# Issuing two weight loads earlier on GpSimd in a linear-attention and feed-forward kernel

## The chip, the cores and the metric

The kernel runs on one core of a Trainium2 chip. The metric is the time of one execution on the device, in microseconds, as the median of several runs. A profiled execution has two numbers: its own time, and its span, which goes from the first instruction's start to the last one's end.

## The reference, cut to what matters

Linear attention with decay runs over 4 batches, 8 heads, 768 positions and head size 64, in blocks of 64 positions that hand a 64x64 state from one to the next. Its output, taken as 3072 tokens of 512 values, goes through a feed-forward layer with a leaky gate.

```python
for b in range(nb):                      # blocks of 64 positions
    intra = np.einsum('bhic,bhjc->bhij', qb, kb) * Dmask[None]
    intra = np.einsum('bhij,bhjd->bhid', intra, vb)
    inter = np.einsum('bhid,bhde->bhie', qb * lam_pow[None], kv_state)
    out[:, :, sl] = intra + inter
    kb_dec = kb * rev_pow[None]
    kv_state = lam_block[None, :, None, None] * kv_state + np.einsum('bhsd,bhse->bhde', kb_dec, vb)
...
h = x @ w_in                             # x: 3072 x 512, w_in: 512 x 2048
g = np.maximum(h, 0.0) + alpha * np.minimum(h, 0.0)
return (g @ w_out).astype(np.float32)    # w_out: 2048 x 512
```

## The kernel before, in words

**Units and chunks.** The tokens are worked on in six chunks `c`. A chunk holds 256 positions of two batches (`bi` 0 and 1), so 512 tokens. The attention of a chunk is cut into four units, one for each batch and each half of the heads (`hh`). Units are numbered through: units 0 to 3 belong to chunk 0, units 4 to 7 to chunk 1, and so on. "The third and fourth unit" are units 2 and 3.

**What a unit does.** `turn` transposes queries and keys on TensorE, `turned` copies them out of PSUM, `decayed` multiplies queries by the decay, `key_decayed` makes the decayed keys, `cast` makes 16-bit copies of the keys or queries. `cluster(old, new)` is a burst of small matmuls: scores and state increments of the new unit, outputs of the old one. `masked` multiplies the scores by the decay mask on VectorE. `aged` (L686, always on GpSimd) multiplies a state by its decay into the tile `old`, and `state` (L675 on ScalarE or L677 on VectorE) adds the increment. `out_of` (on ScalarE) copies the attention output of a unit into `xT`, the input of the feed-forward layer.

**The feed-forward layer.** `up(c, f, bi, slot)` makes 128 of the 2048 hidden values for the tokens of a chunk: four matmuls (L705) into one of three PSUM banks; `bi` other than None takes half of the tokens. `below` (L716, ScalarE) and `gate` (L728, VectorE) turn the bank into the tile `g`, and only then is the bank free for a later `up`. `down` (L738) multiplies `g` by `w_out_sb`.

**Loads.** Three queues issue transfers. GpSimd issues those that change 32-bit floats to 16-bit ones: the values `vh`, some of the queries `qh`, and the weights, `w_in_sb` by `load_win` (L116) and `w_out_sb` by `load_wout` (L122). In the profile these are queue q0, software_dynamic. SyncE issues the keys `kraw` and some queries in 32 bits (L83); they are queue q1, hardware_dynamic. ScalarE issues the stores of the output. `load_win(c0, n)` brings n columns of `w_in`, for `up` with f from c0/128 on. `load_wout(f0, n)` brings n of the sixteen blocks of 128 rows of `w_out`. `hold` is a tiny VectorE write into a key tile, which makes the load of this tile wait until VectorE has reached that point.

**The order.** The program is a list written out by hand, one call after another, from line 771 to line 1164; from there a loop weaves the remaining chunks together. Each engine takes its own instructions in the order of this list and waits at the first that is not ready. Around the change GpSimd's order before is: `aged(1, 1)`, `decayed(3)`, `aged(9, 0)`, `aged(2, 1)`, `aged(10, 0)`, `aged(3, 1)`, `load_win(1536, 512)`, `aged(11, 0)`, `load_wout(0, 4)`, `load16("q", 1, 0)`, `load16("v", 2, 0)`, `key_decayed(5)`, `load16("v", 1, 0)`, `key_decayed(4)`, `key_decayed(6)`, and further loads. SyncE issues the keys of chunk 1, `load("k", 1, 0)` for units 4 and 5 and `load("k", 1, 1)` for units 6 and 7, behind `hold("k", 1, 0)` at line 854. Their first readers outside GpSimd are `cast(4, "k", "A")` on ScalarE (line 909), `cast(5, "k", "V")` on VectorE (line 911) and `cast(6, "k", "A")` on ScalarE (line 921), each of which stands among the `below` and `gate` calls of chunk 0.

Of the kernel before, what the change touches and what calls it, by code (L numbers as in the profile page):

```python
# [11 lines left out]
def kernel(  # L12
# [102 lines left out]
    def load_win(c0, n):  # L115
        nc.gpsimd.dma_start(  # L116
            out=w_in_sb[:, :, ds(c0, n)],
            in_=moe_w_in[:, ds(c0, n)].rearrange("(g p) f -> p g f", p=128),
        )

    def load_wout(f0, n):
        nc.gpsimd.dma_start(  # L122
            out=w_out_sb[:, ds(f0, n), :],
            in_=moe_w_out[ds(f0 * 128, n * 128), :].rearrange("(f p) d -> p f d", p=128),
        )
# [111 lines left out]
    def mask_of(hl, hh):  # L237

        m = dmask[:, hl, ds(2 * hh, 2)]
        x = [list(y) for y in m.ap]  # L240
        return bass.AP(tensor=m.tensor, offset=m.offset, ap=[x[0], x[1], [64, 2], [1, L]])
# [124 lines left out]
    def bank(slot, name):  # L366
        return ps.tile([128, CH], fp32, tag=f"b{slot}", name=name)
# [84 lines left out]
    def turn(n):  # L452

        t = T[n]
        tp = t["tp"] = ps.tile([128, 2, 2, 2, L], fp16, tag="tk", name="tp")
        for x in (1, 0):
            src = half(n, "qk"[x])
            for e in range(2):
                for hp in range(2):
                    if x == 1 or "qk16" in t:  # L460
                        nc.tensor.transpose(  # L461
                            tp[:, x, e, hp, :], src[:, e, ds(2 * hp, 2)].rearrange("p l d -> p (l d)"), ident
                        )
                    else:
                        for hl in range(2):
                            nc.tensor.transpose(  # L466
                                tp[ds(hl * 64, 64), x, e, hp, :], src[:, e, hp + 2 * hl], ident
                            )
# [145 lines left out]
    def masked(n, hl=None):  # L614
        t = T[n]
        hh = units[n][2]
        if hl is not None:
            t.setdefault("sm", {})[hl] = sm_pool.tile([128, 2, 2, L], fp16, tag=f"sm{hl}", name=f"sm{hl}")
            nc.vector.tensor_tensor(  # L619
                out=t["sm"][hl],  # L620
                in0=t["s"][:, hl].rearrange("p (h x j) -> p h x j", h=2, x=2),
                in1=mask_of(hl, hh),
                op=ALU.mult,
            )
        else:

            t["sm"] = sm_pool.tile([128, 2, 2, L], fp16, tag="sm0", name="sm0")
            nc.vector.tensor_tensor(
                out=t["sm"],
                in0=t["s"][:, :, 0 : 4 * N].rearrange("p l (e x) -> p l e x", e=2),  # L630
                in1=nmask[:, ds(4 * hh, 4)]
                .rearrange("p (l h) j -> p l (h j)", l=2)
                .unsqueeze(2)
                .to_broadcast([128, 2, 2, 2 * N]),
                op=ALU.mult,
            )

    def out_of(n, eng="A"):
        c, bi, hh = units[n]
        if c not in XT:  # L640
            XT[c] = xt_pool.tile([128, NHP, 2, 2, L], fp16, tag="xT", name="xT")
        x = XT[c][:, ds(2 * hh, 2), :, bi, :].rearrange("p h e (a j) -> p a (h e) j", a=2)
        if T[n]["acc"] is not None:
            copy_on(eng, x, T[n]["acc"][:, :, 0:256].rearrange("p a (he j) -> p a he j", j=64))
        else:
            for a in range(2):
                copy_on(eng, x[:, a], T[n]["part"][a][:, 0:256].rearrange("p (he j) -> p he j", j=64))


    def follows(n, a):  # L650

        c, bi, hh = units[n]
        step = L // N if c < FIRST else 1
        b, i = 2 * (c % 2) + bi, 4 * (c // 2) + a * step
        if (b, hh, i + step) not in R:
            state_tile(b, hh, i + step)
        return R.get((b, hh, i)), R.get((b, hh, i + step))

    def state(n, a):
        before, then = follows(n, a)  # L660
        c, bi, hh = units[n]
        if then is None:
            return
        if c >= FIRST:
            for hp in range(2):
                nc.vector.scalar_tensor_tensor(  # L666
                    out=then[:, hp, :],
                    in0=before[:, hp, :],
                    scalar=nrdecay[:, 2 * hh + hp : 2 * hh + hp + 1],
                    in1=T[n]["kv"][a % 2][:, a // 2, hp, :],  # L670
                    op0=ALU.mult,
                    op1=ALU.add,
                )
        elif before is None:
            nc.scalar.activation(then, T[n]["kv"][a][:, 0], AF.Copy)  # L675
        else:
            nc.vector.tensor_tensor(out=then, in0=T[n]["kv"][a][:, 0], in1=T[n]["old", a], op=ALU.add)  # L677

    def aged(n, a):

        before, then = follows(n, a)
        if then is None:
            return
        hh = units[n][2]
        x = T.setdefault(n, {})["old", a] = half_pool.tile([128, 2, D], fp32, tag=f"old{a}", name=f"old{a}", bufs=4)
        nc.gpsimd.tensor_tensor(  # L686
            out=x,
            in0=before,
            in1=rdecay[:, ds(2 * hh, 2)].unsqueeze(2).to_broadcast([128, 2, D]),
            op=ALU.mult,  # L690
        )
# [8 lines left out]
    def up(c, f, bi, slot):  # L700
        n = CH if bi is None else W
        h_ps = HP[c, f, bi] = bank(slot, "h_ps")
        for gi in range(NHP):
            x = XT[c][:, gi]
            nc.tensor.matmul(  # L705
                h_ps[:, 0:n] if bi is None else h_ps[:, 0:n].rearrange("p (e j) -> p e j", e=2),
                lhsT=w_in_sb[:, gi, ts(f, 128)],
                rhs=x.rearrange("p e b j -> p (e b j)") if bi is None else x[:, :, bi, :],
                start=(gi == 0),
                stop=(gi == NHP - 1),  # L710
            )

    def below(c, f, bi):
        n = CH if bi is None else W
        m = M[c, f, bi] = m_pool.tile([128, CH], fp32, tag="m", name="m")
        nc.scalar.activation(m[:, 0:n], HP[c, f, bi][:, 0:n], AF.Relu, scale=-1.0)  # L716

    def gate(c, f, bi):
        n = CH if bi is None else W
        if (c, f) not in G:  # L720
            G[c, f] = g_pool.tile([128, 2, 2, L], fp16, tag=f"g{f}", name=f"g{f}")
        g, m, h_ps = G[c, f], M.pop((c, f, bi)), HP.pop((c, f, bi))
        if bi is None:
            g, mv, hv = g.rearrange("p e b j -> p (e b j)"), m, h_ps
        else:
            g = g[:, :, bi, :]
            mv, hv = (y[:, 0:n].rearrange("p (e j) -> p e j", e=2) for y in (m, h_ps))
        nc.vector.scalar_tensor_tensor(  # L728
            out=g, in0=mv, scalar=oma[:, f : f + 1], in1=hv, op0=ALU.mult, op1=ALU.add
        )  # L730
# [115 lines left out]
    aged(8, 0)  # L846
    state(1, 0)
    aged(1, 1)
    masked(1, 1)
    turn(3)  # L850
    fill(2)
# [18 lines left out]
    cluster(2, 3, True)  # L870
    gate(0, 0, 0)
    aged(10, 0)
    up(0, 1, 0, 2)
    out_of(2, "A")
    masked(3, 0)
# [3 lines left out]
    gate(0, 1, 0)  # L879
    aged(3, 1)  # L880
    cluster(3, None)
    load_win(1536, 512)
    state(3, 1)
    up(0, 2, 0, 2)
    out_of(3, "A")
# [1 line left out]
    aged(11, 0)  # L887
    below(0, 2, 0)
    up(0, 0, 1, 1)
    load_wout(0, 4)  # L890
    below(0, 3, 0)
    gate(0, 2, 0)
    below(0, 0, 1)
# [401 lines left out]
```

## Time and profile before

| | |
|---|---|
| median of 3 runs | 221.33 us (219.97 to 222.4) |
| the profiled execution's own time | 221.9 us |
| its span | 220.1 us, so 1.8 us lie around it |
| mean granted TensorE clock | 0.988 |
| TensorE busy | 211.8 us (96%) |
| VectorE, ScalarE, GpSimd busy | 127.1, 111.6, 95.9 us |
| DMA | 28.44 MB; q0 35.6% and q1 31.0% of the sixteen engines' time |

The profile is of one execution. Times in timelines count from the start of the span. The share of TensorE is nearly the whole span, so a change is worth only what it does to the few waits of TensorE, and to its clock. The DMA engines are full for the first 70 us, which is where the two moved loads lie; after that they have room.

### The profile page before, as it was taken

Reading aid. Unit: us, or ns where it says so; the run is one execution under the profiler, and the core shown is the slowest. Engines: PE = TensorE matmul, PEld = TensorE weight load, DVE = VectorE, ACT = ScalarE, POOL = GpSimd, SP = SyncE. Lnnn points to the kernel's source line nnn. Section 1 sums busy time; section 2 is a strip of 40 time slices with the busy share of each in tenths; the row PEclk is TensorE's granted clock in tenths of the full one; section 3 lists DMA queues with packets and bytes.
Section 4 is the critical chain, followed back from the end, with each engine's and each line's share of the span. In section 5 each row is a group of like instructions: output and inputs, shape, how many; then the busy total and the mean of one; then the engine's idle time right before and its main releaser. Section 6 shows DMA issues by size and latency. Waiting matters only on the chain.

```text
span 220.1 us, 5893 instructions
## 1 busy us (share of the span) xinstructions
PE 211.8 (96%) x2463; PEld 114.6 (52%) x2463; DVE 127.1 (58%) x260; ACT 111.6 (51%) x209; POOL 95.9 (44%) x146
## 2 busy tenths in 40 slices
PE   8988899899999999999999999999999999999992
PEld 8777544556665545454545444444444444444461
DVE  3988577666887787464667566556755254443000
ACT  4762585744655564646664545555445434443120
POOL 7874796553998770776596243620100000000000
PEclk9999699999999999999999999999999999999998
DMA  4999999999998599299269995236011001100221
GB/s 118 244 193 232 192 159 183 202 171 196 299 229 199 85 219 118 74 184 172 74 89 217 180 229 130 64 82 71 27 51 48 17 35 48 48 38 13 95 92 53
DMA packets 71194, 28.44 MB, mean 129 GB/s; under 512 B 52080, under 2 KB 68224, under 8 KB 71168
## 3 DMA queue, kind: packets, MB, share of 16 engines
q0 software_dynamic: 26592, 8.65, 35.6%
q1 hardware_dynamic: 40800, 13.11, 31.0%
q10 hardware_dynamic: 3776, 6.31, 8.0%
q8 instruction: 19, 0.31, 0.6%
q14 instruction: 7, 0.06, 0.1%
HBM read 27.28 MB, written 6.29 MB: 153 GB/s over the span
## 4 chain that ended last, share of the span: by engine, by line
PE 91%; ACT 2%; DVE 2%; POOL 2%; issue 1%; POOLq 0%
PE h_ps L705 38%; PE o_ps L738 32%; PE o_ps L760 6%; PE acc L538 3%; PE s L586 2%; PE op_fill L380 2%; PE acc L558 2%; PE tp L466 2%; PE tp L461 1%; PE acc L603 1%; ACT qkT L392 1%; PE mk_ps L267 1%; POOL vh L83 0%; PE s L603 0%; DVE less L245 0%
## 5 line engine op out<-in xcount | busy, mean ns | idle before, releaser
L728 DVE SCALAR_TENSOR_TENSOR g<-m,oma,h_ps 128x512 f16<-128x512 f32 (+1 forms) x106 | 73.2, 696 | 64.9 <-ACT m L716 63.5
L705 PE MATMUL h_ps<-xT,w_in_sb 128*128 128x512 f16 (+1 forms) x424 | 98.1, 364 | 0.2
L716 ACT ACTIVATE m<-h_ps 128x512 f32<-128x512 f32 (+1 forms) x106 | 59.0, 557 | 57.4 <-PE h_ps L705 55.5
L738 PE MATMUL o_ps<-w_out_sb,g 128*128 128x512 f16 x320 | 81.2, 379 | 0.0
L705 PEld LDWEIGHTS <-w_in_sb 128*128 128x128 f16 x424 | 40.4, 99 | 41.1 <-issue 1.2
L738 PEld LDWEIGHTS <-g 128*128 128x128 f16 x320 | 30.9, 98 | 35.8
L749 ACT ACTIVATE o_sb<-o_ps 128x512 f32<-128x512 f32 (+1 forms) x25 | 14.5, 580 | 18.8 <-PE o_ps L760 11.1
L619 DVE TENSOR_TENSOR sm<-s,dmask 128x512 f16<-128x512 f32 x32 | 21.2, 683 | 1.8 <-PE s L586 1.8
L392 ACT ACTIVATE xT<-acc 128x512 f16<-128x512 f32 x22 | 13.1, 597 | 16.8 <-PE acc L558 9.6
L686 POOL TENSOR_TENSOR old<-R,rdecay 128x128 f32<-128x128 f16 x24 | 9.6, 408 | 26.3 <-DVE R L677 15.7
L444 POOL TENSOR_TENSOR kdec<-kraw,kdecay 128x256 f16<-128x256 f32 x30 | 18.4, 638 | 1.5 <-DMA kraw<-in_k_dram 0.8
L494 POOL TENSOR_TENSOR qdT<-qkT,nqdecay 128x512 f16<-128x512 f16 x8 | 9.3, 1165 | 21.5 <-DMA qkT<-qk 17.8
L494 POOL TENSOR_TENSOR qdT<-qkT,qdecay 128x512 f16<-128x512 f16 (+1 forms) x12 | 12.0, 1003 | 6.0 <-ACT qkT L392 3.0
L760 PE MATMUL o_ps<-w_out_sb,g 128*128 128x512 f16 (+1 forms) x80 | 14.0, 336 | 0.0
L380 PE MATMUL op_fill<-filler 128*128 128x128 f16 x122 | 10.7, 258 | 1.1 <-DVE sel L203 1.1
L538 PE MATMUL acc<-qdT,R 64*64 64x64 f16 (+1 forms) x216 | 10.9, 217 | 0.9 <-ACT R L675 0.7
L760 PEld LDWEIGHTS <-g 128*128 128x128 f16 x80 | 7.8, 98 | 6.2
L538 PEld LDWEIGHTS <-R 64*64 64x64 f16 x224 | 5.9, 104 | 9.5 <-issue 6.3
L666 DVE SCALAR_TENSOR_TENSOR R<-R,nrdecay,s 128x64 f16<-128x64 f16 x48 | 10.4, 275 | 0.0
L380 PEld LDWEIGHTS <-filler 128*128 128x128 f16 x122 | 9.3, 119 | 1.6 <-DVE sel L203 1.1
L586 PE MATMUL s<-qkT 64*64 64x128 f16 (+1 forms) x384 | 9.3, 210 | 0.9 <-issue 0.5
L558 PE MATMUL acc<-sm,vh 64*64 64x128 f16 (+1 forms) x352 | 8.5, 211 | 0.0
(98 smaller groups left out, 159.5 us busy)
## 6 DMA issues: line engine op xcount, KB each, us to landing
out_dram<-o_sb ACTq DMA_DIRECT2D x23, 256.0 KB, 2.1
kraw<-in_k_dram SPq DMA_DIRECT2D x12, 256.0 KB, 5.1
kraw<-in_k_dram SPq DMA_DIRECT2D x6, 512.0 KB, 8.0
qraw<-in_q_dram SPq DMA_DIRECT2D x10, 256.0 KB, 6.6
vh<-in_v_dram POOLq DMA_DIRECT2D x8, 256.0 KB, 9.4
w_out_sb<-in_moe_w_out_dram POOLq DMA_DIRECT2D x4, 512.0 KB, 8.3
w_in_sb<-in_moe_w_in_dram POOLq DMA_DIRECT2D x3, 512.0 KB, 10.4
qh<-in_q_dram POOLq DMA_DIRECT2D x5, 256.0 KB, 9.0
```

Of the source, the lines that this page charges most:

```text
L380: nc.tensor.matmul(t[:, 0:128], lhsT=filler, rhs=filler, start=True, stop=True)
L392: nc.scalar.activation(out, in_, AF.Copy)
L444: engine(eng).tensor_tensor(out=kdec[:, e], in0=kr[:, e], in1=kdecay[:, ds(4 * hh, 4), e].unsqueeze(2).to_broadcast([128, 4, D]), op=ALU.mult,
L494: engine(eng).tensor_tensor(out=out, in0=src, in1=(qdecay if c < FIRST else nqdecay)[:, hh].rearrange("p e h j -> p (e h) j").unsqueeze(2) ...
L538: nc.tensor.matmul(o, lhsT=before[ds(hl * 64, 64), hp, :], rhs=x, start=not own and e == 0, stop=False, skip_group_check=True,)
L619: nc.vector.tensor_tensor(out=t["sm"][hl], in0=t["s"][:, hl].rearrange("p (h x j) -> p h x j", h=2, x=2), in1=mask_of(hl, hh), op=ALU.mult,)
L705: nc.tensor.matmul(h_ps[:, 0:n] if bi is None else h_ps[:, 0:n].rearrange("p (e j) -> p e j", e=2), lhsT=w_in_sb[:, gi, ts(f, 128)], rhs=x ...
L716: nc.scalar.activation(m[:, 0:n], HP[c, f, bi][:, 0:n], AF.Relu, scale=-1.0)
L728: nc.vector.scalar_tensor_tensor(out=g, in0=mv, scalar=oma[:, f : f + 1], in1=hv, op0=ALU.mult, op1=ALU.add)
L738: nc.tensor.matmul(O[c, t], lhsT=G[c, f][:, t // 2, t % 2, :], rhs=w_out_sb[:, f, :], start=(f == 0), stop=(f == NF - 1),)
L749: nc.scalar.activation(o_sb[:, 0:n], o_ps[:, 0:n], AF.Copy)
L760: nc.tensor.matmul(o_ps[:, 0:n], lhsT=G[c, f][:, t // 2, t % 2, :], rhs=w_out_sb[:, f, ts(x, n)], start=(f == 0), stop=(f == NF - 1),)
```

## The change

Two calls move up in the list. `load_win(1536, 512)`, the last quarter of `w_in`, goes from behind `cluster(3, None)` to behind `aged(1, 1)`: GpSimd issues it ahead of `decayed(3)`, `aged(9, 0)`, `aged(2, 1)`, `aged(10, 0)` and `aged(3, 1)`. `load_wout(0, 4)`, the first quarter of `w_out`, goes from behind `up(0, 0, 1, 1)` to behind `aged(10, 0)`: it is issued ahead of `aged(3, 1)` and `aged(11, 0)`. Among the loads that GpSimd issues the order stays as it was. SyncE's list is not changed, but the loads of the keys of chunk 1, at lines 856 and 859, now come behind the issue of the last quarter of `w_in`.

```diff
     state(1, 0)
     aged(1, 1)
+    load_win(1536, 512)
     masked(1, 1)
     turn(3)
...
     gate(0, 0, 0)
     aged(10, 0)
+    load_wout(0, 4)
     up(0, 1, 0, 2)
...
     cluster(3, None)
-    load_win(1536, 512)
     state(3, 1)
     up(0, 2, 0, 2)
     out_of(3, "A")
...
     up(0, 0, 1, 1)
-    load_wout(0, 4)
     below(0, 3, 0)
```

## The prediction

> **What bounds the kernel now.** I read the page first. TensorE is busy for 96% of the span and holds 91% of the chain that ended last:
>
> ```profile
> span 220.1 us, 5893 instructions
> PE 211.8 (96%) x2463; PEld 114.6 (52%) x2463; DVE 127.1 (58%) x260; ACT 111.6 (51%) x209; POOL 95.9 (44%) x146
> DMA  4999999999998599299269995236011001100221
> PE 91%; ACT 2%; DVE 2%; POOL 2%; issue 1%; POOLq 0%
> ```
>
> So a load can only gain or cost what TensorE waits. Then the timeline of GpSimd around the two moved calls (start, duration, line, tiles, and in brackets the idle time before and what ended it):
>
> ```profile
> 16.54 0.40 POOL L686 TENSOR_TENSOR old<-R,rdecay 128x128 f32<-128x128 f16 x1 [0.96 <-ACT R L675]
> 18.65 0.67 POOL L494 TENSOR_TENSOR qdT<-qkT,qdecay 128x256 f16<-128x256 f16 x1 [1.70 <-DVE qkT L394]
> ...
> 20.58 0.40 POOL L686 TENSOR_TENSOR old<-R,rdecay 128x128 f32<-128x128 f16 x1 [0.40 <-DVE R L677]
> 23.21 0.40 POOL L686 TENSOR_TENSOR old<-R,rdecay 128x128 f32<-128x128 f16 x1 [2.23 <-ACT R L675]
> 23.56 0.80 POOL L116 DMA_DIRECT2D w_in_sb<-in_moe_w_in_dram  x1
> ...
> 24.73 0.80 POOL L122 DMA_DIRECT2D w_out_sb<-in_moe_w_out_dram  x1
> ```
>
> The reader is to see two holes, of 1.70 and 2.23 us, just where the issues go, and their old places. Third, the readers of the keys of chunk 1, on SyncE's, ScalarE's and VectorE's timelines:
>
> ```profile
> 17.96 1.00 SPq L83 DMA_DIRECT2D kraw<-in_k_dram  x2
> 28.68 0.62 ACT L392 ACTIVATE k<-kraw 128x512 f16<-128x512 f32 x1
> 31.70 0.62 ACT L392 ACTIVATE k<-kraw 128x512 f16<-128x512 f32 x1
> 29.22 0.42 DVE L394 CAST k<-kraw 128x512 f16<-128x512 f32 x1
> ```
>
> None has a bracket, so none waits. The two key loads landed at 24.70 and 26.40.
>
> **The change, step by step.**
>
> *GpSimd's time.* An issue takes 0.80 us (0.77 to 0.96 over the five of L116). The first now runs from 16.94 to 17.74 and `decayed(3)` needs the copy that ends at 18.57, so 0.8 us are spare. The second runs from 20.98 to 21.78, and `aged(3, 1)` is released at about 23.2, so 1.4 us are spare. Queued behind them are the state operations whose results VectorE takes at 20.21 and 23.65; both are reached in time. Cost nothing; the cover is GpSimd's waits for VectorE and ScalarE. Without it each issue would cost 0.8 us, 1.6 in all.
>
> *VectorE beside the issue.* One price is not shown directly. The same operation of VectorE took 1.88 us beside GpSimd's kdec work and 0.42 us beside an idle GpSimd:
>
> ```profile
> 13.45 1.88 DVE L494 TENSOR_TENSOR qdT<-qkT,qdecay 128x256 f16<-128x256 f16 x1
> 17.52 0.42 DVE L494 TENSOR_TENSOR qdT<-qkT,qdecay 128x256 f16<-128x256 f16 x1
> ```
>
> The second of these now starts while the issue runs until 17.74. It can lose nothing, or at most the 0.22 us of overlap; the cast at 29.22 overlapped an issue that ended at 29.37 and still took 0.42, so I take 0. The Trainium skill ("SBUF — State Buffer", on the shared port pair) goes further: GpSimd cannot write a transfer's descriptors while VectorE holds that pair in a two-port mode. By it the issue, not VectorE, would be late, by about one 0.42 us operation, and 0.8 us are spare: the sum stays.
>
> *Weights that come sooner.* The last quarter of `w_in` landed at 29.22 and is first read at about 34 (`up(0, 12)`); the quarter of `w_out` landed at 33.24 and is read at 36.2. TensorE has no wait at either. Gain nothing.
>
> *Who shares the DMA engines.* Here the cost can arise. Before, q0 was nearly empty from 22 to 25, and the two key loads (q1, 1 MB) had the engines alone: on the middle engine the first landed at 23.0 and the second at 24.7, so 64 packets took 1.7 us, 27 ns each. The last engine was 1.7 us behind. Now `w_in`'s quarter (issued 16.94) is queued when the keys arrive, and `w_out`'s (20.98) behind it. How do two full queues share? In 48 to 51 us both were full:
>
> ```profile
> q0 software_dynamic: 786, 0.24, 73.6%
> q1 hardware_dynamic: 770, 0.39, 60.7%
> ```
>
> 786 packets against 770: one for one. On the last engine at 21.7 to 22.8, weight packets of 1024 B alternating with key packets are 115 ns apart in the trace, against 80 ns alone (the third and fourth load of `w_in`, 32 packets per engine each: landed 2.6 us apart on the middle engine). The Trainium skill ("DMA: Bandwidth & Descriptors", section SWDGE vs HWDGE vs iDMA) says that an engine takes its queues in turn; by that, the trace agrees with it at 48 to 51 us, and the sum is the one that follows.
>
> *The sum, with one for one.* The keys' packets start at about 20.4 (2.4 us behind their issue). In q0 stand 7 left packets of the third quarter per engine, then 32 of `w_in`'s fourth: 39 pairs x 0.115 = 4.5 us, to 24.9. The first key load needs 25 more pairs, now with `w_out`. That quarter's packets came slower before: on the middle engine it landed 3.55 us behind `w_in`'s, 111 ns for each of 32 packets, 31 more than 80: 25 x 0.146 = 3.65, to 28.5, and 1.7 for the last engine: landed at 30.2. ScalarE's cast stands at 28.68: **1.5 us late**. Behind it in ScalarE's queue stand `below(0, 4)` and all further ones; TensorE has three banks and in this stretch starts an `up` as soon as a bank is free (36 matmuls in 7.98 us, no slack), so TensorE loses the 1.5. The second key load needs 7 x 0.146 = 1.0 and then 57 packets beside the 256-byte packets of q and v, at 62 ns (3 us over 49 pairs per engine in 48 to 51): 3.5. That is 33.0, with the last engine 34.7. The cast at 31.70 has moved to 33.2: **1.5 more**, of which I count 1.1, since the q and v loads are issued from 24.4 on and part of the packets then pass alone. Sum 2.6 us. From the other side: if the keys keep the engines, 0; if q0 goes wholly first (both quarters, q and v: 20.8 + 2 x 2.6 + 2 x 1.43 = 28.9, then 1.7 + 1.1), the first lands at 31.7 and costs 3.0, with nothing more for the second.
>
> *What is late next.* GpSimd's `key_decayed(5)` waits for the same keys: 30.2 instead of 27.29, so the loads behind it are issued 2.9 us later. The `w_out` quarters that landed at 43.40 and 45.99 are read at 45.6 and 49.1; with TensorE 2.6 later and q0 emptier they are still in time. `decayed(4)` at 39.84 finds GpSimd done at 36.88 + 2.9. No further cost.
>
> *The clock.* The busy times of TensorE in stretches, with the granted clock and then the DMA share as the last columns:
>
> ```profile
> 16.90:20.30 3.40, 3.34 (x91) 2.69 (x88) 3.15 (x9) 0.77 (x2) 1.47 (x4) 1.00 1.25 209
> 20.30:23.70 3.40, 2.15 (x74) 1.46 (x76) 2.51 (x6) 1.49 (x5) 0.89 (x3) 1.00 1.15 293
> 23.70:27.10 3.40, 3.40 (x33) 2.36 (x22) 1.20 (x3) 1.65 (x4) 3.38 (x5) 0.50 0.77 136
> ```
>
> After a stretch in which TensorE was busy 2.15 of 3.40 the clock was halved for 3.4 us; after 2.85 of 3.50 (13.4 to 16.9) it wasn't. A new stall of 1.1 to 1.5 us leaves 1.9 to 2.3 busy if it falls into one stretch. That would cost 1.7 us more (half of 3.4). I leave it out of the sum and keep it for the range.
>
> So the profiled execution would be 221.9 + 2.6 = 224.5. The median of the runs is 0.6 below the profiled execution; on its scale 221.3 + 2.6 = **223.9 us**.
>
> **The rivals.**
>
> *Hidden (not slower).* Transfers are served in order of issue. For it: at the start the landings follow the issues, and at 8.5 to 9.5 q1 moved 646 packets to q0's 38 although q0 had loads outstanding. Then only `w_in`'s quarter goes ahead of the keys, 2.6 us; they land at 27.3 and 29.0, before 28.68 and 31.70. It decides as long as the first lands before about 28.8. Against it: the 786 to 770. Time 221.3, or 221.0 with the 0.3 us that VectorE's cast waits for a key load at 54.30, as the hole in the DMA at 24.5 to 25.7 is filled.
>
> *Keys late and the clock halved.* As the forecast, plus one stretch at half clock: 223.9 + 1.7 = 225.6. For it: the 2.15 row. Against it: the stall comes in two parts, on both sides of a stretch's end.
>
> *The halved stretch goes away.* A small shift around 20 to 24 us could keep the clock up at 23.7. The sixteen matmuls from 24.11 took 3.33 us; at full clock VectorE's `gate` (0.48 each, four) would set the pace, 1.9: a gain of 1.4, so 219.9. The change removes no wait there, so little speaks for it; the runs before differ by 2.4 us, which such a stretch could explain.
>
> *The issues hold GpSimd up.* If each delayed the states by its whole length: 222.9. The holes of 1.70 and 2.23 us speak against it.
>
> **How the numbers follow.** Keys late, with or without the clock: 0.45 for the two together (0.3 and 0.15). Hidden: 0.35. GpSimd held up: 0.05. Halved stretch gone: 0.15. A measurement of this kernel can tell about 1%, 2.2 us, from no change. Slower by more than that: the late keys and a little from scatter, 0.47. Faster by more: most of the last case stays within 1%, so 0.13 with what I can't see. Within 1%: 0.40. The range goes from 219.7, the halved stretch gone, to 225.7, the keys late and the clock halved; the forecast's own range is 222.5 to 225.7.
>
> **What would show it.** Right: both issues in the holes; `decayed(3)` still at 18.6; ScalarE's cast of keys with a wait for a DMA in its bracket, at about 30; the two key loads landing near 30 and 34; TensorE idle between 28 and 34. Wrong: the key loads landing before 28.7 and 31.7, or TensorE's times from 28 us on shifted by less than 1 us, or a shift that begins before 24 us.

## Result and the profile after

The changed kernel takes 223.22 us in the median of 20 runs (221.57 to 224.38), the kernel before 220.88 us in the median of 20 (219.97 to 222.4), 2.3 us less. The means are 222.9 and 221.0 us, 1.9 us apart, and the ratio over all these runs is 1.008, with a 95% interval of 1.0062 to 1.0098: slower, by a little under 1%. The medians lie further apart because the runs of the changed kernel fall into two groups, near 221.7 and near 223.4 us. Two of the experiments below had one run each in a slower state (226.26 and 226.35 us), which their medians and ratios leave out.

The profiled execution took 223.22 us with a span of 221.4, against 221.9 and 220.1 before, 1.3 us more in the spans. Both profiled executions have one stretch of 3.4 us at half clock from 23.7 us on. Many other runs have a mean clock too high for such a stretch, and that is where the larger difference of the medians comes from (below). A load is spread over sixteen DMA engines that finish at different times: "landed" without more means on the last of them, which the readers wait for, and "on the middle engine" means on the eighth.

The page of the kernel after, its span, busy times and the chain that ended last:

```profile
span 221.4 us, 5893 instructions
PE 211.9 (96%) x2463; PEld 114.6 (52%) x2463; DVE 126.6 (57%) x260; ACT 111.5 (50%) x209; POOL 96.1 (43%) x146
PE 84%; DMA 9%; DVE 3%; ACT 1%; issue 1%; POOL 0%; SPq 0%; ACTq 0%
PE h_ps L705 34%; PE o_ps L738 31%; DMA kraw<-in_k_dram 7%; PE o_ps L760 6%; PE acc L538 3%; PE s L586 2%; DMA lam_sb<-in_lam_dram 2%; PE acc L558 2%; PE tp L466 2%; PE tp L461 1%; PE op_fill L380 1%; ACT qkT L392 1%; PE acc L603 1%; PE mk_ps L267 1%; DVE sm L619 1%
```

TensorE has the same work, 211.9 us, but the chain now goes through a DMA for 9% of the span, 7% of it the keys. Before, no DMA was on it. GpSimd's timeline around the moved issues:

```profile
16.57 0.80 POOL L116 DMA_DIRECT2D w_in_sb<-in_moe_w_in_dram  x1
18.35 0.66 POOL L494 TENSOR_TENSOR qdT<-qkT,qdecay 128x256 f16<-128x256 f16 x1 [0.97 <-DVE qkT L394]
...
20.61 0.80 POOL L122 DMA_DIRECT2D w_out_sb<-in_moe_w_out_dram  x1
23.19 0.39 POOL L686 TENSOR_TENSOR old<-R,rdecay 128x128 f32<-128x128 f16 x1 [1.77 <-ACT R L675]
...
29.40 1.35 POOL L444 TENSOR_TENSOR kdec<-kraw,kdecay 128x256 f16<-128x256 f32 x2 [3.25 <-DMA kraw<-in_k_dram]
```

Both issues lie in the holes, and GpSimd still waits 0.97 and 1.77 us behind them for VectorE and ScalarE. New is the last line: 3.25 us of waiting for keys. ScalarE's and TensorE's timelines show how it gets to the end; first TensorE before, without a gap in this stretch, and then both after:

```profile
24.04 12.35 PE L705 MATMUL h_ps<-xT,w_in_sb 128*128 128x256 f16 x60
```

```profile
29.28 0.63 ACT L392 ACTIVATE k<-kraw 128x512 f16<-128x512 f32 x1 [0.59 <-DMA kraw<-in_k_dram]
33.19 0.63 ACT L392 ACTIVATE k<-kraw 128x512 f16<-128x512 f32 x1 [1.42 <-DMA kraw<-in_k_dram]
35.14 2.75 PE L705 MATMUL h_ps<-xT,w_in_sb 128*128 128x512 f16 x12 [1.16 <-DVE g L728]
```

The two casts that had no bracket before wait for the key loads, which landed at 29.26 and 33.17 (24.70 and 26.40 before). One bank later TensorE stands still for 1.16 us, because `gate`, and `below` ahead of it, came late. Matmul by matmul, TensorE is 0.03 us ahead of the kernel before at 29.5 us, 0.2 behind from 31 on, and 1.5 behind from 34 on; 0.15 come back near 57 us. That is the 1.3 us of the spans.

### The profile page after: what moved, and what is told of

It is laid out like the page before. It is cut to its first block, busy times and chain, and to the rows that moved or that the text cites. A ratio compares the mean times of both kernels' runs of the same rounds, so it can differ in the third digit from the quotient of the medians.

```text
span 221.4 us, 5893 instructions
## 1 busy us (share of the span) xinstructions
PE 211.9 (96%) x2463; PEld 114.6 (52%) x2463; DVE 126.6 (57%) x260; ACT 111.5 (50%) x209; POOL 96.1 (43%) x146
## 3 DMA queue, kind: packets, MB, share of 16 engines
q1 hardware_dynamic: 40800, 13.11, 30.2%
HBM read 27.28 MB, written 6.29 MB: 152 GB/s over the span
## 4 chain that ended last, share of the span: by engine, by line
PE 84%; DMA 9%; DVE 3%; ACT 1%; issue 1%; POOL 0%; SPq 0%; ACTq 0%
PE h_ps L705 34%; PE o_ps L738 31%; DMA kraw<-in_k_dram 7%; PE o_ps L760 6%; PE acc L538 3%; PE s L586 2%; DMA lam_sb<-in_lam_dram 2%; PE acc L558 2%; PE tp L466 2%; PE tp L461 1%; PE op_fill L380 1%; ACT qkT L392 1%; PE acc L603 1%; PE mk_ps L267 1%; DVE sm L619 1%
```

## Experiments

Four theories. **Late keys**: the early weights and the keys share the DMA engines, the keys land late, and what waits for them in the order of an engine delays TensorE. **Issue time**: the 0.8 us on GpSimd ahead of the states is what costs. **Order of issue**: transfers are served as issued, so the keys can't be delayed beyond `w_in`'s quarter. **Clock**: the loss is a matter of half-clock stretches.

**One load alone.** Two kernels, each with one of the two moves.

```diff
+    load_win(1536, 512)          # first kernel: behind aged(1, 1)
+    load_wout(0, 4)              # second kernel: behind aged(10, 0)
```

> Only the last quarter of w_in is issued early; the quarter of w_out stays at its old place. Late keys (the weights' transfers slow the keys, the keys' casts hold ScalarE, ScalarE holds TensorE): w_in's 32 packets per engine pass one for one with the keys until about 25, then the keys pass nearly alone; the key loads land near 27.5 and 30, before their casts at 28.7 and 31.7, so no wait and the time of before, 220.9 us (within 0.5). If the cost were the issue of w_in on GpSimd ahead of the states, half or more of the 2.3 us would show, 222 us or more. If any early weight load slows the keys enough: ScalarE waits for the second load at about 31.7 and the time is near 222.

> Only the quarter of w_out is issued early; the last quarter of w_in stays at its old place, so w_out goes ahead of it in the queue. Late keys: the first key load lands near 26, before its cast; the second has to share with w_out and then with w_in and lands near 33, so ScalarE waits about 1.4 us at the cast of the sixth unit's keys and the time is 222.3 to 223.2 us. If transfers are served in order of issue, the keys (issued 3 us before w_out) land as before at 24.7 and 26.4 and the time is 220.9. If GpSimd's issue time is the cost: aged(3, 1) starts later than 23.2 and the time is above 221.5 with no wait for a DMA on ScalarE.

Measured: 221.0 us, ratio 1.0004 (0.9982 to 1.0025), and 220.87 us, ratio 0.9999 (0.9978 to 1.002). Neither move costs anything; only together do they. With `w_in` alone the key loads landed at 27.7 and 29.4, as forecast from the packets (27.5 and 30): from 22 to 23.5 us the two queues passed 211 and 212 packets, one for one. The first cast waited a little:

```profile
27.73 0.63 ACT L392 ACTIVATE k<-kraw 128x512 f16<-128x512 f32 x1 [0.75 <-DMA kraw<-in_k_dram]
29.95 0.62 ACT L392 ACTIVATE k<-kraw 128x512 f16<-128x512 f32 x1
```

With `w_out` alone they landed at 24.3 and 26.0, as order of issue would have it, where I had expected the second at 33: a miss. The quarter of `w_out`, issued at 21.38, landed on the middle engine at 27.2, 2.4 us behind the second key load. That is about what its 32 packets there take alone (80 ns each, as in the prediction), so on this engine it passed behind the keys and not among them. Part of this is start-up. In the kernel before with the later start (below), the last quarter of `w_in` was issued at 27.28 while the DMA engines stood idle: no packet moved from 26 to 28.5 us, 13 from 28.5 to 29.5, and 80 in the half microsecond after that.

```profile
q0 software_dynamic: 13, 0.01, 44.1%
```

So most engines began some 2.2 us behind the issue. For the `w_out` issued at 21.38 that is about 23.6, when the first key load had landed on most engines and a little under half of the second was left. Even then it did not share one for one: from 23.5 to 24.5 us it moved 56 packets to the keys' 426.

**The issues without the bytes.** The kernel before, with two small loads at the new places.

```diff
+    def small_load(w, name):
+        t = const.tile([128, 4, 16], fp16, name=name)
+        nc.gpsimd.dma_start(out=t, in_=w[ds(0, 512), 0:16].rearrange("(g p) f -> p g f", p=128))
...
     aged(1, 1)
+    small_load(moe_w_in, "s_in")
...
     aged(10, 0)
+    small_load(moe_w_out, "s_out")
```

> The kernel before, with two small loads (128 x 4 x 16 values each, into tiles that nobody reads) issued by GpSimd at the two new places, and the real weight loads at their old places. GpSimd spends its issue time (about 0.8 us each) as in the changed kernel, while almost no bytes move. Late keys: no cost, the two key loads land near 25 and 27, time 220.9 us (within 0.5). If the issue time on GpSimd is what costs: 223.2 us, with decayed(3) or aged(3, 1) later than 18.6 and 23.2.

Measured: 220.99 us, ratio 1.0011 (0.9991 to 1.0031), keys at 24.4 and 26.1, the issues 0.80 and 0.81 us long. Issue time is out.

**Where the late keys hurt.** In the changed kernel, first the casts on ScalarE and VectorE are moved down, then GpSimd's own work on the keys as well, then that alone.

```diff
# first: the casts
-    cast(4, "k", "A")            # to behind below(0, 10)
-    cast(5, "k", "V")            # to behind gate(0, 11)
-    cast(6, "k", "A")            # to behind below(0, 12)
# second: the casts, and this; third: this alone
-    key_decayed(5, "G")
...
     load16("v", 1, 1)
+    load_wout(4, 4)
+    load_wout(8, 4)
+    key_decayed(5, "G")
+    key_decayed(4, "G")
+    key_decayed(6, "G")
+    cast(7, "k", "G")
+    key_decayed(7, "G")
```

> The changed kernel, with the three casts of the keys of units 4, 5 and 6 on ScalarE and VectorE moved down by some 6 us (behind below(0, 10), gate(0, 11) and below(0, 12)). The keys stay late. Late keys by way of ScalarE's order: the key loads still land near 29.3 and 33.2 and GpSimd still waits for them, but neither ScalarE nor VectorE does; TensorE has no gap at 34 and the time is that of before, 220.9 us (within 0.6), perhaps a little less. If the time goes by the clock or by GpSimd, or if the keys are late for the transposes at 38 as well: 223.2 us, as in the changed kernel.

> The changed kernel with the three casts moved down as in the run before, and with GpSimd's work on the keys (key_decayed of units 4 to 7 and one cast) moved behind all its loads up to the third quarter of w_out, so that no load waits behind the late keys. Late keys by two ways (ScalarE's casts, and GpSimd's loads of w_out that stand behind its own work on the keys): with both ways closed TensorE waits neither at 34 nor at 45 us, and the time is that of before or a little under it, 220.3 to 221.2 us. If a third thing costs (the early issue itself, the clock, the transfers as such): 222.5 us or more.

> The changed kernel with only GpSimd's work on the keys moved behind its loads; the casts on ScalarE and VectorE stay at their old places. Late keys by two ways: ScalarE still waits at the cast of the sixth unit's keys until about 33, TensorE has its gap at 34 to 35 and the time stays near 223 us (222.3 to 223.4). If only the late w_out loads cost: 220.9 us.

With the casts moved: 222.71 us, ratio 1.0059 (1.0031 to 1.0088). The casts wait no more and the gap at 34 is gone, but the time hardly falls: my first expectation missed. TensorE's timeline tells where most of it went:

```profile
46.26 1.02 PE L738 MATMUL o_ps<-w_out_sb,g 128*128 128x512 f16 x4 [1.33 <-DMA w_out_sb<-in_moe_w_out_dram]
53.70 1.02 PE L738 MATMUL o_ps<-w_out_sb,g 128*128 128x512 f16 x4 [0.49 <-DMA w_out_sb<-in_moe_w_out_dram]
```

The second and the last quarter of `w_out` are late, 1.8 us in the two waits; the runs at a mean clock of 0.995 or more lie 2.4 us above those of the kernel before (223.3 against 220.9), so a part is not accounted for. GpSimd issues the second quarter behind its own work on the keys, at 38.32 instead of 35.32. In the changed kernel this didn't show, since TensorE was late by itself. With both ways closed: 221.12 us, ratio 1.0019 (0.9998 to 1.0041), no different from before within the interval, although the keys land at 29.2 and 33.2 as in the changed kernel. With GpSimd's part alone: 223.27 us, ratio 1.0103 (1.0069 to 1.0138), with ScalarE and TensorE as follows:

```profile
29.27 0.63 ACT L392 ACTIVATE k<-kraw 128x512 f16<-128x512 f32 x1 [2.21 <-DMA kraw<-in_k_dram]
33.43 0.63 ACT L392 ACTIVATE k<-kraw 128x512 f16<-128x512 f32 x1 [2.07 <-DMA kraw<-in_k_dram]
31.22 2.75 PE L705 MATMUL h_ps<-xT,w_in_sb 128*128 128x512 f16 x12 [1.71 <-DVE g L728]
35.38 2.75 PE L705 MATMUL h_ps<-xT,w_in_sb 128*128 128x512 f16 x12 [1.41 <-DVE g L728]
```

So late keys are the cause, by two ways, each of which is enough: ScalarE's order and GpSimd's. One control is lacking: the same calls were not moved in the kernel before, so it is not shown that moving them gains nothing by itself. In the stretch of the stall there is nothing to gain, since TensorE was busy 7.98 of 8.00 us in the kernel before. Busy times from 28.4 to 36.4 us (TensorE first), of the changed kernel and of the one with both ways closed:

```profile
28.40:36.40 8.00, 6.74 (x30) 2.91 (x30) 5.42 (x9) 4.81 (x10) 6.51 (x10) 1.00 1.27 152
```

```profile
28.40:36.40 8.00, 8.00 (x40) 3.59 (x39) 6.96 (x10) 5.75 (x11) 6.94 (x12) 1.00 1.65 192
```

**Both quarters early, but behind the keys.**

```diff
     aged(1, 1)
-    load_win(1536, 512)
...
     aged(10, 0)
+    load_win(1536, 512)
     load_wout(0, 4)
```

> Both quarters are issued early, but behind the keys: load_win(1536, 512) and load_wout(0, 4) stand together behind aged(10, 0), at about 20.6 us, three us after SyncE's issue of the keys. The same bytes move early as in the changed kernel. If what counts is that the software queue never ran empty ahead of the keys (as against the runs with one quarter alone): the queue is empty at 21 to 22, the keys land near 24.5 and 26, and the time is 220.9 us (within 0.4). If the two queues share packet for packet whenever both have work: the second key load lands near 32 or later and the time is 222 us or more.

Measured: 221.58 us, ratio 1.0021 (0.9998 to 1.0043); the keys landed at 24.2 and 25.9. The keys came as forecast, the time missed the forecast 220.9 by 0.7, and the interval just holds no change. What lies above is a matter of the clock: the runs at a mean clock of 0.995 or more have a median of 220.5 us here and in the kernel before measured beside it, but they are 4 of 12 here and 17 of 23 there. Whether the change makes such runs rarer, so few runs don't tell. The packets of the two queues, here from 23 to 24 us, and in the changed kernel from 26 to 28.5 us:

```profile
q1 hardware_dynamic: 517, 0.26, 103.6%
q0 software_dynamic: 24, 0.02, 14.6%
```

```profile
q0 software_dynamic: 342, 0.35, 82.9%
q1 hardware_dynamic: 342, 0.17, 35.4%
```

In both stretches the software queue had a quarter of weights outstanding, issued 2.3 us before the first stretch and 5.4 us before the second. The start-up of 2.2 us was over, or nearly so, when the first stretch began. In the changed kernel the queue shared packet for packet; here it moved next to nothing until the keys were done, and its first quarter landed on the middle engine at 27.0, 2.3 us behind them. That it matters whether the queue had run empty when the new load reached it fits these kernels, but it is argued and not shown. Even the changed kernel had a pause: from 24.5 to 25 us, behind `w_in` and with `w_out` issued 3.9 us before, the software queue moved 17 packets to the keys' 288, and it shared again once the first key load was through on most engines (408 to 406 from 25.5 to 28.5 us). The Trainium skill ("DMA: Bandwidth & Descriptors", section SWDGE vs HWDGE vs iDMA) has an engine take its queues in turn; 342 to 342 agrees, and 24 to 517 does not, unless the new load's packets were not ready by then, which no run here settles.

**A later start.** 95 instead of 50 filler matmuls at the start, in the changed kernel and in the one before.

```diff
-    fill(50)
+    fill(95)
```

> The changed kernel with 95 instead of 50 filler matmuls at the start, so that TensorE reaches its first real matmul some 1.7 us later while the first transfers start as before. To be held against the next run, which has the same in the kernel before. If the cost is a race between transfers and the casts that read the keys: the key loads land near 33 at the latest as before, the cast of the sixth unit's keys now comes at about 33.4, so little or no wait is left and the two kernels are within 0.7 us of each other, both near 222.5. If the change costs by something that moves along with the work (issue time, the order on GpSimd): this one is 2 us or more above the next.

> The kernel before with the same 95 filler matmuls: 1.7 us above the kernel before, about 222.5 us, if the start is on the chain that sets the end; no wait for keys.

Measured: 223.12 us (five runs) and 223.16 us (six runs), ratios to the kernel before of 1.0102 (1.0071 to 1.0133) and 1.0095 (1.0067 to 1.0122). The change costs nothing that these few runs can tell. The two kernels agree as forecast, but not for the reason forecast: I expected late keys and later casts, and the keys were not that late. They landed at 26.8 and 29.1. The second issue came only at 24.16, and the software queue had drained (`w_in` had landed at 24.4 on the middle engine) before its packets could follow; on the middle engine `w_out` again landed 2.2 us behind the second key load. The start itself cost more than forecast, since TensorE now also stood 1.7 to 1.8 us at about 20 us, waiting for nothing that the profile shows.

**The half clock.** The kernel before, with 11 fillers where TensorE waits at 22.5 us.

```diff
+    fill_turned(11)              # into the bank of the transposes
     cluster(3, None)
```

> The kernel before with 11 filler matmuls (0.6 us at full clock) where TensorE waits for ScalarE ahead of the outputs of the fourth unit, at 22.5 to 23.2 us. If the half clock of 23.7 to 27.1 follows from TensorE's idle share in the stretch before: the executions with a mean clock of 0.992 become rare and the median falls by 0.1 to 0.6 us, to 220.3 to 220.8. If the fillers delay the outputs or the clock goes by something else: 220.9 us or more.

Measured: 221.0 us, ratio 0.9999 (0.9976 to 1.0022); 4 of 12 runs have a mean clock of 0.992 or less, against 6 of 17 of the kernel before. The fillers did raise TensorE's busy time, to 2.76 of the 3.40 us from 20.3 on. No gain: a miss. Nothing here beats the kernel before.

**The changed kernel twice more.**

> The changed kernel once more, for a second profile. Its runs fall into two groups, near 221.6 us (mean clock 0.992) and near 223.4 us. If this profile has no stretch at half clock at 23.7 us: TensorE comes to the casts 1.3 us sooner, the keys land at the same 29.3 and 33.2, ScalarE waits about 2 us at each cast and TensorE's gaps near 30 and 34 sum to about 3 us; time 223.4. If it falls into the group near 221.6: the half clock lies at the start (about 8 us), the work comes to the loads later, the software queue runs empty ahead of w_out and the keys land near 27 and 29.

> The changed kernel a third time, with the same two expectations as the run before it; the two together should show which of the two groups goes with which place of the half clock.

One run each. Both fell into the upper group, 223.61 and 223.71 us, with no half-clock stretch before the end. ScalarE and TensorE in the first:

```profile
29.11 0.63 ACT L392 ACTIVATE k<-kraw 128x512 f16<-128x512 f32 x1 [1.72 <-DMA kraw<-in_k_dram]
33.59 0.63 ACT L392 ACTIVATE k<-kraw 128x512 f16<-128x512 f32 x1 [2.39 <-DMA kraw<-in_k_dram]
31.06 2.75 PE L705 MATMUL h_ps<-xT,w_in_sb 128*128 128x512 f16 x12 [1.23 <-DVE g L728]
35.54 2.75 PE L705 MATMUL h_ps<-xT,w_in_sb 128*128 128x512 f16 x12 [1.73 <-DVE g L728]
```

At full clock ScalarE reaches the casts sooner, but the keys land no sooner, and TensorE waits 1.23 + 1.73 = 3.0 us instead of losing 1.5. So what the full clock saves is lost again in waiting. Over the 20 runs of the result, those with a mean clock of 0.995 or more have a median of 223.4 (11 runs). The kernel before has 220.9 in such runs (20 of the 35 runs measured beside the first experiments) and 221.6 in the others. Of the other nine runs of the changed kernel, three lie at 223.2 to 223.6 and six at 221.6 to 221.8, where the change costs almost nothing. None of those six was profiled. A half-clock stretch at the start, as in the profile of the small loads (8.05 to 11.46 us), would act like the later start; that is argued and not shown.

## Why the prediction was right or wrong

**GpSimd's time: right.** Cost nothing; 0.97 and 1.77 us of waiting are left behind the issues, and the small loads confirm it. **VectorE beside the issue: right.** The operation overlapped only the last 0.17 us of the issue and took 0.42 us again (17.20 to 17.62). The issue was not late either: it took 0.80 us (16.57 to 17.37) with VectorE busy all along. No run here shows what an issue does beside a two-port mode of VectorE.

**Weights that come sooner: right.** No wait of TensorE went away.

**Sharing: right in kind, mis-sized, and right in part by luck.** The key loads were forecast for 30.2 and 34.7 and landed at 29.26 and 33.17. The sum had the first one done at 28.5 on the middle engine and 1.7 us later on the last; it was done at 25.7 on the middle engine and 3.5 us later on the last, and these two errors nearly cancel. The step that failed is the one that let `w_out` share with the first key load from 24.9 on, on every engine. On thirteen of the sixteen that load had landed by 26.5, and there `w_out` passed beside the second one. On the other three it landed at 28.2 to 29.3, as late as the forecast needs, and the cast waits for all sixteen. The term for a pair with a `w_out` packet, 146 ns, should have been 117 (342 pairs on sixteen engines in 2.5 us), about the 115 of the other weights.

In the profiled execution the sum of 2.6 us measured 1.5, less 0.15 given back later: 223.22 us instead of the 224.5 forecast for it. The second wait, forecast at 1.1 net, made nearly all of it (1.42 on ScalarE), the first, forecast at 1.5, only 0.59. That the median nevertheless moved by 2.3 us, close to the sum, is luck: I took the profiled execution with its half-clock stretch as the base, and in the two profiled runs without one ScalarE reaches the casts earlier and TensorE waits 3.0 us. The forecast of 223.9 also stood on a median of three runs, 221.33; twenty runs gave 220.88.

**One for one as a rule: too simple.** It held where I had read it, in the changed kernel from 25.5 us on, and with `w_in` alone (211 to 212 packets). It did not hold in the kernels where `w_out` came alone, or both quarters came behind the keys: there the keys had the engines nearly to themselves, first because a new load needs some 2.2 us to start and then for a reason that stays open. The rival "hidden", order of issue, gives the right landings for the kernels with one early quarter (27.3 and 29.0 for `w_in` alone, measured 27.7 and 29.4), though with `w_in` alone the packets went one for one and not in order; it does not describe the changed kernel.

**What is late next: right here, with less to spare than I wrote.** The second quarter of `w_out` was in time (landed 45.88, read at 47.1) because TensorE was late; with the casts out of the way TensorE waited 1.33 us for it.

**The clock: wrong.** I kept 1.7 us for a second stretch at half clock after the stall. There was none. The first stretch, at 23.7, stayed in the profiled execution, with TensorE busy 1.88 of 3.40 before it. In the stretch of the stall TensorE was busy 2.24 of 3.40, hardly more than the 2.15 of the kernel before, and the granted clock stayed at 1.00:

```profile
20.30:23.70 3.40, 1.88 (x70) 1.25 (x64) 2.34 (x5) 1.33 (x5) 1.51 (x3) 1.00 1.20 212
23.70:27.10 3.40, 3.40 (x32) 2.34 (x23) 1.16 (x3) 1.75 (x4) 2.17 (x3) 0.51 1.19 246
33.90:37.30 3.40, 2.24 (x12) 0.97 (x11) 2.53 (x4) 2.21 (x5) 3.38 (x6) 1.00 0.82 78
```

The first of the two further profiles goes lower still, with 1.68 of 3.41 in the second stall, and the stretch behind it is at full clock too:

```profile
33.57:36.98 3.41, 1.68 (x9) 0.68 (x7) 2.06 (x3) 2.47 (x5) 3.25 (x5) 1.00 0.75 73
36.98:40.39 3.41, 3.41 (x27) 1.70 (x24) 2.24 (x3) 1.41 (x3) 2.96 (x5) 1.00 1.31 127
```

So the busy share of TensorE in a stretch, from which I took this term, does not decide alone whether the clock is halved. What does is open.

## What to carry to other kernels

An early issue can cost more than its issue time: look up which other transfers are due in the next ten microseconds, and in which engine's order their readers stand. Here 1 MB of weights with 3 to 5 us to spare got among 1 MB of keys with 4 to 5 us to spare, and a 0.6 us cast in the middle of the feed-forward work carried the delay to TensorE. When one wait is removed and the time stays, look for a second reader of the same late data: here GpSimd's own work on the keys held back the next weights.

## What the runs showed of the hardware

A load that GpSimd issued into an empty software queue, beside idle DMA engines, had its packets under way on most engines some 2.2 us after the issue (issued at 27.28, 13 packets by 29.5, 80 in the next half microsecond). Beside a hardware queue that had work lined up, such a load moved still less after that time: 24 packets to 517 in the microsecond from 23 us on, 2.3 to 3.3 us behind its issue. With one quarter of weights right behind another the two queues shared packet for packet, 342 to 342, after a pause of about half a microsecond (17 to 288). Why is open; no run separates how a queue's packets are fetched from how the engines choose.

Stretches at half clock before the end of the span were 3.41 us long in every profile that has one and lay at different places, 23.7 us in the kernel before and 8.05 us in the one with small loads. Runs of the kernel before with a mean clock below 0.995 took 0.7 us more than the others (221.6 to 220.9); where their stretches lay was not profiled. A stretch with TensorE busy 2.15 of 3.40 us was followed by half clock, one with 1.68 of 3.41 was not. Eleven fillers in one wait did not measurably make such runs rarer (4 of 12 against 6 of 17).
